# Attention scores as three products of halves, a weight conversion held behind attention's tail, and the experts' raw tiles in other places

## The chip, the core and the metric

The kernel runs on one core of a Trainium2 chip. TensorE (PE) multiplies, VectorE (DVE) and ScalarE (ACT) do the element-wise work and copy results out of PSUM, GpSimd (POOL) and SyncE (SP) mostly issue DMAs. The metric is the device time in microseconds (us): 786.6 us as the median of three runs (786.15 to 787.62).

## The reference

All inputs are float32. Three parts follow one another:

```python
scores = scale * np.matmul(q, k.transpose(0, 1, 3, 2))      # q, k, v: 2 x 12 heads x 448 x 64
scores = np.einsum('bhij,hg->bgij', scores, w_pre)          # heads are mixed before the softmax
attn = np.exp(scores - np.max(scores, axis=-1, keepdims=True))
attn = attn / (np.sum(attn, axis=-1, keepdims=True) + 1e-09)
attn = np.einsum('bhij,hg->bgij', attn, w_post)             # and after it
x = np.matmul(attn, v)                                      # as 896 tokens x 768
xn = x / np.sqrt(np.mean(x * x, axis=-1, keepdims=True) + 1e-06) * rms_g
x = (silu(xn @ w_gate) * (xn @ w_val)) @ w_out              # 768 -> 1536 -> 768
e_idx = np.argmax(x @ w_gate2, axis=1)                      # one of 8 experts for each token
out[mask] = gate_w * eom * (np.maximum(x[mask] @ w1[e], 0.0) @ w2[e])   # 768 -> 1024 -> 768
```

The weights of the feed-forward part (`w_gate`, `w_val`, `w_out`) arrive as float64 and are turned into float32 with bit operations on the chip.

## The kernel before

**Attention.** Each batch has four chunks of 120, 110, 110 and 108 query rows, eight chunks in all. A chunk's scores come from `qk` (L157): for a pair of heads, two f32 products of 64 rows each, one on each half of PE's rows, into two PSUM banks, and copies to the tile `s`. There are 48 pairs. The scores are then cut into blocks of 10 query rows x 12 heads: a DMA (`shuffle`, L166, tile `d`, 210 KB, six buffers) lays the 120 rows of a block on the partitions, on SP's queue for even blocks and on POOL's for most odd ones. There are 90 blocks. For block m, `pre` mixes the heads (L172, PE), takes the maximum (L176, DVE), `soft` exponentiates (L182, ACT), `weigh` folds the sum into the second mixing matrix `w` (L189 to L191, DVE), and `post` of block m-2 multiplies by `w` (L202, PE). Shuffles are issued five blocks ahead. The products with v (`av`, L216), the preparation of later chunks (`q_part`, `k_pair`: transposes on PE and copies) and the steps of the norm fill in the blocks. A block in the first six of a chunk also carries one pair of scores of the next chunk. The first two chunks' scores are made ahead of block 0, in `prologue`. The table `loads` says in which block each DMA of v of batch 0 (`v`, 12 heads in six parts) and of k of batch 1 is issued, on POOL's queue.

**Beside attention.** `at(m, f)` puts a step behind block m. In blocks 57 to 78 the first two columns of 128 of `w_gate` and `w_val` are loaded (L488, tile `raw`), converted by steps on DVE (L489, L490, L494) and ACT (L493), and split into a high part (fp32r, a cast on ACT, L526) and a low part (the rest, a subtraction on DVE, L527). In block 79 the third column is loaded (`load_2`), and its conversion is written behind `a.run()`; in blocks 83 to 86 the first four chunks' x are split (L475, L476). The attention itself is issued in the order written (`manual_schedule`); what stands behind it is ordered by the scheduler, which may move it ahead into attention's last blocks. `tail` is the order of what remains after the last block.

**Feed-forward part.** Every product there is made three times in fp32r, high x high, high x low, low x high (`mm3`, L502 to L504). x's two groups of 448 tokens meet 12 columns in `ffn1`; `ffn2` takes token tiles of 128 through `w_out`. `route` chooses the expert, writes the token's row to DRAM by expert, and `first_x` (L776, L784) builds the first expert's x from rows already there and from the last tile.

**Experts.** Each expert's weights are eight raw tiles of 768 KB, fetched on SP's queue (L849), cast to `wh` on ACT (L865), the rest to `wl` on DVE (L866), and used by `mm1` and `mm2` through `mm3`. `transpose_x` (L827 to L829) makes the next expert's x. The pools of raw tiles (`self.raws`) lie over memory of the feed-forward part: a tile can be fetched once its old owner is done.

## Time and profile before

| | us |
|---|---|
| median of three runs (lowest, highest) | 786.6 (786.15, 787.62) |
| the profiled execution | 786.7 |
| its span in the trace | 785.0 |
| PE busy | 730.8 (93%) |
| DVE busy | 479.8 (61%) |
| ACT busy | 387.5 (49%) |
| mean granted clock of TensorE | 0.975 |

Stage by stage: chunks 1 and 2 ahead of the blocks end at 27.7 us, attention's blocks start there, the first product of the feed-forward part is at 298.2 us, its last at 583.5, the experts follow to 785.0. The engines' shares are means over all these. A timeline row gives the start, the duration of a group of instructions, and in brackets how long the engine stood idle before them and what ended that. Rows of a matmul in f32 count two records for each instruction.

### The profile page before, as it was taken

To read this page: it belongs to the slowest core of one execution; us is meant where nothing else is said; L and a number is where in the kernel's file an instruction comes from. 1 tells how busy PE (TensorE), PEld (TensorE's weight loads), DVE (VectorE), ACT (ScalarE), POOL (GpSimd) and SP (SyncE) were. 2 spreads that over 40 slices of the span, in tenths; PEclk is the share of its full clock that TensorE was granted. 3 is DMA by queue.
4 is the path that set the end of the run, shared out by engine and by line. 5 is a ranking of instruction groups with operands and counts; after the bars stand their busy time and mean duration, and the time that the engine had idled before them with its cause. 6 is when DMAs were issued, how large, how long until landed. Compare 5 with 4: busy or idle time off the path is not lost.

```text
span 785.0 us, 11939 instructions
## 1 busy us (share of the span) xinstructions
PE 730.8 (93%) x4414; PEld 596.0 (76%) x4414; DVE 479.8 (61%) x1016; ACT 387.5 (49%) x679; POOL 78.0 (10%) x133
## 2 busy tenths in 40 slices
PE   7889999999998759999999998999988799999994
PEld 4456575665645538999999998999986688988894
DVE  3555667566775775788888823032106889778750
ACT  3455656556565453534334512232215777778661
POOL 5133100121001000000000000011000000020010
PEclk9999999999999799999999999999998899999998
DMA  8577755667566404795554000131159999999100
GB/s 136 105 157 147 121 73 82 120 121 173 86 145 113 86 5 161 205 284 195 185 176 163 1 1 0 45 138 61 41 192 387 378 380 381 380 342 355 58 25 17
DMA packets 83434, 122.02 MB, mean 155 GB/s; under 512 B 20915, under 2 KB 63559, under 8 KB 83375
## 3 DMA queue, kind: packets, MB, share of 16 engines
q1 hardware_dynamic: 75471, 98.05, 42.8%
q0 software_dynamic: 6752, 20.05, 12.3%
q10 hardware_dynamic: 1152, 3.15, 1.1%
q8 instruction: 36, 0.59, 0.3%
q14 instruction: 23, 0.19, 0.1%
HBM read 90.51 MB, written 12.21 MB: 131 GB/s over the span
## 4 chain that ended last, share of the span: by engine, by line
PE 66%; DMA 11%; DVE 9%; issue 7%; ACT 5%; POOL 0%; SPq 0%; POOLq 0%; DVEq 0%; ACTq 0%
PE ps_po L202 7%; PE ps_pm L172 6%; PE ps_pm L504 5%; PE ps_pm L502 5%; PE ps_pm L503 5%; PE ps_po L504 5%; PE ps_po L503 5%; PE ps_po L502 5%; PE ps_qk L157 4%; PE ps_av L216 4%; PE ps_qk L503 3%; PE ps_qk L504 3%; PE ps_qk L502 3%; DMA d<-s 3%; DMA xe<-ys 2%
## 5 line engine op out<-in xcount | busy, mean ns | idle before, releaser
L202 PEld LDWEIGHTS ps_po<-w,p 120*112 120x112 f32 x720 | 84.7, 180 | 68.6 <-issue 41.9
L866 DVE TENSOR_TENSOR wl<-raw,wh 128x1536 fp32r<-128x1536 f32 x64 | 110.9, 1754 | 28.2 <-ACT wh L865 28.1
L202 PE MATMUL ps_po<-w,p 120*112 120x120 f32 x720 | 94.9, 276 | 18.4 <-DVE w L191 17.1
L182 ACT ACTIVATE p<-ps_pm,mx 120x448 f32<-120x448 f32 x90 | 57.1, 634 | 102.9 <-DVE mx L176 62.0
L865 ACT CAST wh<-raw 128x1536 fp32r<-128x1536 f32 x64 | 93.0, 1481 | 7.6 <-PE ps_pm L504 4.7
L172 PE MATMUL ps_pm<-d,a_kpre 120*120 120x448 f32 x180 | 86.8, 564 | 4.9 <-DMA d<-s 4.9
L176 DVE TENSOR_REDUCE mx<-ps_pm 120x1 f32<-120x448 f32 x90 | 56.0, 622 | 49.7 <-PE ps_pm L172 49.0
L493 ACT ACTIVATE raw<-raw 128x768 f32<-128x768 f32 x36 | 33.0, 922 | 70.8 <-DVE raw L490 64.0
L204 ACT COPY at<-ps_po 112x480 f32<-112x480 f32 x90 | 50.9, 566 | 3.3 <-PE ps_po L202 1.1
L157 PE MATMUL ps_qk<-kt,qt 64*110 64x448 f32 (+2 forms) x192 | 52.1, 589 | 0.5 <-ACT qt L88 0.2
L503 PE MATMUL ps_po<-wl,hh 128*128 128x384 f32 x144 | 49.4, 343 | 0.3 <-DVE wl L866 0.2
L502 PE MATMUL ps_po<-wh,hh 128*128 128x384 f32 x144 | 49.2, 342 | 0.0
L504 PE MATMUL ps_po<-wh,hl 128*128 128x384 f32 x144 | 48.6, 340 | 0.1
L502 PE MATMUL ps_pm<-wh,xh 128*128 128x512 f32 x108 | 44.9, 416 | 3.0 <-ACT xh L828 2.2
L166 POOL DMA_DIRECT2D d<-s x42 | 24.7, 589 | 218.5 <-PE ps_pm L172 173.6
L504 PE MATMUL ps_pm<-wh,xl 128*128 128x512 f32 x108 | 44.1, 410 | 2.2 <-DVE xl L829 2.2
L216 PE MATMUL ps_av<-at,v 112*64 112x110 f32 (+2 forms) x768 | 45.0, 264 | 1.2 <-ACT at L204 0.7
L503 PE MATMUL ps_pm<-wl,xh 128*128 128x512 f32 x108 | 44.4, 411 | 1.5 <-DVE wl L866 1.5
L597 DVE TENSOR_TENSOR hl<-h,hh 128x1536 fp32r<-128x1536 f32 (+2 forms) x9 | 12.3, 1400 | 48.6 <-ACT hh L596 24.6
L216 PEld LDWEIGHTS ps_av<-at,v 112*64 112x64 f32 x768 | 37.0, 137 | 6.0 <-ACT at L204 0.9
L88 DVE COPY s<-ps_qk 110x448 f32<-110x448 f32 (+2 forms) x48 | 29.8, 622 | 14.8 <-PE ps_qk L157 13.8
L157 PEld LDWEIGHTS ps_qk<-kt,qt 64*110 64x110 f32 (+2 forms) x192 | 15.3, 174 | 30.5 <-issue 22.6
(258 smaller groups left out, 1589.1 us busy)
## 6 DMA issues: line engine op xcount, KB each, us to landing
raw<-in_moe_w_dram SPq DMA_DIRECT2D x64, 768.0 KB
d<-s SPq DMA_DIRECT2D x48, 210.0 KB
raw<-in_moe_w_gate_dram SPq DMA_DIRECT2D x12, 768.0 KB
raw<-in_moe_w_val_dram SPq DMA_DIRECT2D x12, 768.0 KB
raw<-in_moe_w_out_dram SPq DMA_DIRECT2D x12, 768.0 KB
d<-s POOLq DMA_DIRECT2D x42, 210.0 KB, 5.6
ys<-z SPq DMA_DIRECT2D x8, 385.0 KB
v<-in_v_dram POOLq DMA_DIRECT2D x12, 224.0 KB, 6.5
```

What stands on the lines that cost most here:

```text
L157: nc.tensor.matmul(pss[e][:ni], lhsT=self.qt[n][e * D:(e + 1) * D, p, :ni], rhs=self.kt[b, p][e * D:(e + 1) * D, :], start=True, stop=True,)
L172: self.marks[m, "p"] = nc.tensor.matmul(ps, lhsT=self.kpre.rearrange("p i g -> p (i g)"), rhs=self.dt.pop(m), start=True, stop=True).ins
L176: self.marks[m, "v"] = nc.vector.tensor_reduce(mx, ps, axis=AX.X, op=ALU.max, negate=True).ins
L182: self.nc.scalar.activation(p, ps, AF.Exp, bias=mx, scale=1.0, accum_out=sm)
L202: nc.tensor.matmul(ps[:, c], lhsT=p[:, c * CP:(c + 1) * CP], rhs=w, start=True, stop=True)
L204: self.marks[m + self.LP, "a"] = nc.scalar.copy(dst, ps.rearrange("p c h i -> p (c h) i")).ins
L216: nc.tensor.matmul(ps[e * D:(e + 1) * D, j, :ni], lhsT=vt[(g0 + e) // HH][:self.CP, (g0 + e) % HH, c, :], rhs=at[:, c, g0 + e, :ni], start ...
L502: nc.tensor.matmul(ps, lhsT=ah, rhs=bh, start=first, stop=False)
L503: nc.tensor.matmul(ps, lhsT=ah, rhs=bl, start=False, stop=False)
L504: self.last["t"] = nc.tensor.matmul(ps, lhsT=al, rhs=bh, start=False, stop=last).ins
L865: self.nc.scalar.copy(h, raw)
L866: self.last["v"] = self.nc.vector.tensor_sub(l, raw, h.bitcast(F32)).ins
```

## The change

It does seven things. (1) q and k are split into high and low halves when they are transposed (`k_pair`, `q_part`; the low half, a subtraction on DVE, is returned and issued a little later), and `qk` makes three fp32r products for each half of the rows. The low halves of k lie in tiles of `w0`, so the homes of the split weights swap between `nw` and `w0`. (2) v of batch 0 is loaded in blocks 6 to 16, not 0 to 10, and six parts of k of batch 1 in blocks 7 to 17 between them, the rest in 19 to 24. (3) The low halves of the first two weight columns are made one block after the high ones, as are those of x. (4) In `tail` the casts of two chunks stand ahead of their subtractions. (5) The third column's conversion waits until the last x of attention is split. (6) The first products of `first_x` are issued inside the last `route`. (7) The experts' pools are laid out anew: `hi` first, then raw tiles in pools of 1, 2, 2, 2, 4, 2, 1.

```diff
@@ -129,22 +129,29 @@
             )
-        kt = self.kp_.tile([128, self.S], F32, tag="kt", name="kt")
-        self.evict(kt, ps.rearrange("p c j -> p (c j)"))
-        self.kt[b, p] = kt
+        kt = self.kp_.tile([128, self.S], F32R, tag="kt", name="kt")
+        if p % 3 == 0:
+            self.kl = self.klo.tile([128, 1536], F32R, tag="wg" if p == 0 else "wv", name="ktl")
+        kl = self.kl[:, p % 3 * self.S:(p % 3 + 1) * self.S]
+        src = ps.rearrange("p c j -> p (c j)")
+        nc.scalar.copy(kt, src)
+        self.kt[b, p] = kt, kl
+        return lambda: nc.vector.tensor_sub(kl, src, kt.bitcast(F32))
     def q_part(self, n, j, tag="qk"):
...
         if j == 0:
-            self.qt[n] = self.qp.tile([128, self.NP, self.QB], F32, tag="qt", name="qt")
+            self.qt[n] = self.qp.tile([128, 2, self.NP, self.QB], F32R, tag="qt", name="qt", bufs=1)
         ps = self.psum(tag, [128, 3, self.QB])
...
             )
-        self.evict(self.qt[n][:, 3 * j:3 * j + 3, :ni], ps[:, :, :ni])
+        qh, ql = (self.qt[n][:, x, 3 * j:3 * j + 3, :ni] for x in range(2))
+        nc.scalar.copy(qh, ps[:, :, :ni])
+        return lambda: nc.vector.tensor_sub(ql, ps[:, :, :ni], qh.bitcast(F32))
     def qk(self, n, p):
@@ -153,11 +160,13 @@
         pss = [self.psum("qk", [self.QB, self.S]) for _ in range(2)]
-        for e in range(2):
-            nc.tensor.matmul(
-                pss[e][:ni], lhsT=self.qt[n][e * D:(e + 1) * D, p, :ni], rhs=self.kt[b, p][e * D:(e + 1) * D, :],
-                start=True, stop=True,
-            )
+        kh, kl = self.kt[b, p]
+        for x, (a, k) in enumerate(((0, kh), (0, kl), (1, kh))):
+            for e in range(2):
+                sl = slice(e * D, (e + 1) * D)
+                nc.tensor.matmul(
+                    pss[e][:ni], lhsT=self.qt[n][sl, a, p, :ni], rhs=k[sl, :], start=(x == 0), stop=(x == 2),
+                )
         return [lambda e=e: self.evict(self.st[n][:ni, 2 * p + e, :], pss[e][:ni]) for e in range(2)]
...
@@ -252,9 +261,10 @@
         self.prologue()
-        loads = {2 * j: f for j, f in enumerate(self.load_kv(0, "v"))}
-        loads.update({j + 12: f for j, f in enumerate(self.load_kv(1, "k"))})
-        avs, todo, preps = [], [], []
+        loads = {2 * j + 6: f for j, f in enumerate(self.load_kv(0, "v"))}
+        for j, f in enumerate(self.load_kv(1, "k")):
+            loads[2 * j + 7 if j < 6 else j + 13] = f
+        avs, todo, preps, lows = [], [], [], []
         for m in range(NB + LP):
@@ -264,6 +274,9 @@
                 if busy:
+                    for f in lows:
+                        f()
+                    lows = []
                     evicts = self.qk(n + 1, r)
@@ -293,10 +306,13 @@
                             avs.pop(0)()
+                    for f in lows:
+                        f()
+                    lows = []
                     if preps and m < NB and (n or r >= self.NP):
-                        preps.pop(0)()
+                        lows += filter(None, [preps.pop(0)()])
                         if len(preps) > nr - 1 - r:
-                            preps.pop(0)()
+                            lows += filter(None, [preps.pop(0)()])
                 if not avs or busy or end:
@@ -472,8 +488,14 @@
         xh, xl = (self.xs[g][:, j, :, o:o + ni] for j in range(2))
-        nc.scalar.copy(xh, x)
-        nc.vector.tensor_sub(xl, x, xh.bitcast(F32))
+
+        def high():
+            self.last["xa"] = nc.scalar.copy(xh, x).ins
+
+        def low():
+            self.last["xv"] = nc.vector.tensor_sub(xl, x, xh.bitcast(F32)).ins
+
+        return high, low
     def f64_to_f32(self, src, raw, t=None):
@@ -521,14 +543,18 @@
     def split_one(self, fc, f, nm, eng):
-        t = (self.nw if fc % 2 else self.w0).tile([128, 2, self.KD, 128], F32R, tag="w" + nm, name=nm + "hl")
+        t = (self.w0 if fc % 2 else self.nw).tile([128, 2, self.KD, 128], F32R, tag="w" + nm, name=nm + "hl")
         h, l = t[:, 0], t[:, 1]
-        self.nc.scalar.copy(h, f)
-        eng.tensor_sub(l, f, h.bitcast(F32))
-        return h, l
+        return [lambda: self.nc.scalar.copy(h, f), lambda: eng.tensor_sub(l, f, h.bitcast(F32))], (h, l)
...
...
@@ -618,7 +644,7 @@
         return ys
-    def route(self, t, y):
+    def route(self, t, y, beside=None):
         nc, E, rp = self.nc, self.E, self.rp
@@ -629,6 +655,8 @@
             nc.tensor.matmul(lg, lhsT=yT[:, k, :], rhs=self.rw[:, k, :], start=(k == 0), stop=(k == self.KD - 1))
+        if beside:
+            beside()
         v, col = nc.vector, lambda j: m[:, j:j + 1]
@@ -938,8 +966,12 @@
                 for js, some, f, nm in zip(slots, steps, fs, "gv"):
-                    some = some + [lambda f=f, nm=nm: ws[fc].append(self.split_one(fc, f, nm, nc.vector))]
-                    for m, s in zip(js, some):
+                    def split(f=f, nm=nm, m=js[6]):
+                        (high, low), hl = self.split_one(fc, f, nm, nc.vector)
+                        ws[fc].append(hl)
+                        high()
+                        at(m, low)
+                    for m, s in zip(js, some + [split]):
                         at(m, s)
@@ -959,38 +991,48 @@
                     for fc, j, tag in ((0, 0, "qk"), (0, 1, "qk"), (1, 0, "qk"), (1, 1, "pm"))]
-            late = [lambda c=c: self.split_x(c[0] * a.S + c[1], c[2]) for c in a.chunks[-4:]]
+            def late(c):
+                return self.split_x(c[0] * a.S + c[1], c[2])
             def gen():
-                n = 0
                 while todo:
                     yield todo.pop(0)
-                yield lambda: begin_x(1)
-                yield from late[:3]
+                begin_x(1)
+                cs = [late(c) for c in a.chunks[-4:]]
+                yield cs[0][0]
+                yield cs[1][0]
                 yield from avs[:3]
+                yield cs[0][1]
                 yield fill[0]
+                yield cs[1][1]
                 yield from avs[3:]
+                yield cs[2][0]
+                yield cs[2][1]
                 yield fill[1]
-                steps = [s for s in todo]
+                steps = list(todo)
                 k = [s.__name__ for s in steps].index("mean") + 1
...
                 yield from steps[k:]
-                yield late[3]
+                yield from cs[3]
             return gen()
         with ExitStack() as actx:
-            a = Attention(tc, actx, self.psum, self.ident, self.xT, self.nw, sp, self.norm, beside, tail,
+            a = Attention(tc, actx, self.psum, self.ident, self.xT, self.nw, sp, self.w0, self.norm, beside, tail,
                           self.q, self.k, self.v, self.w_pre, self.w_post)
...
             self.NCH = len(a.chunks)
-            at(57, first_weights(0, ((58, 61, 62, 63, 64, 65), (60, 63, 64, 65, 66, 67))))
-            at(68, first_weights(1, ((69, 73, 74, 74, 75, 76), (70, 75, 76, 76, 77, 78))))
+            at(57, first_weights(0, ((58, 61, 62, 63, 64, 65, 66), (60, 62, 63, 64, 65, 66, 67))))
+            at(68, first_weights(1, ((69, 73, 74, 75, 76, 77, 78), (70, 74, 75, 76, 77, 78, 79))))
             at(79, load_2)
...
             for j, c in enumerate(a.chunks[:4]):
-                at(83 + j, lambda c=c: self.split_x(c[0] * a.S + c[1], c[2]))
+                def split(c=c, j=j):
+                    high, low = self.split_x(c[0] * a.S + c[1], c[2])
+                    high()
+                    at(84 + j, low)
+                at(83 + j, split)
             with tc.manual_schedule():
@@ -1009,9 +1051,11 @@
             self.ffn1_out(fc, 0, early[fc, 0], early[fc, 1])
-        for some in raw2.pop():
-            for f in some:
-                f()
+        steps = raw2.pop()
+        with tc.issue_after(self.last["xa"]), tc.issue_after(self.last["xv"]):
+            for some in steps:
+                for f in some:
+                    f()
         self.ffn1(0, 1, ws[0])
@@ -1053,8 +1097,8 @@
         y, = self.ffn2(ts, hs)
-        part = self.first_x(xs[0])
-        self.route(self.TT - 1, y)
+        part = []
+        self.route(self.TT - 1, y, lambda: part.extend(self.first_x(xs[0])))
         self.warm(self.NW[2], self.last["t"])
@@ -1062,12 +1106,10 @@
         m2 = ExitStack()
-        self.raws = []
-        for i, n in enumerate((3, 2, 2, 6, 1)):
-            self.raws += [self.pool(m2, f"raw{i}", n)] * n
-        self.raws = self.raws[7:13] + self.raws[:7] + self.raws[13:]
+        self.hi = self.pool(m2, "hi", self.NHL)
+        self.raws = [[self.pool(m2, f"raw{i}", n)] * n for i, n in enumerate((1, 2, 2, 2, 4, 2, 1))]
+        self.raws = [p for i in (4, 0, 1, 2, 5, 3, 6) for p in self.raws[i]]
         self.nraw = 0
-        self.hi = self.pool(m2, "hi", self.NHL)
         self.xp = self.pool(m2, "xp", 2)
```

On PE, in the blocks of chunk 2 that carry scores of chunk 3 (110 rows), the products of scores stand thus before and after (`kt` and `ktl` are the high and low halves of k; the high and low halves of q are both `qt`):

```order
L157 MATMUL ps_qk<-kt,qt 110x448 x2
L202 MATMUL ps_po<-w,p 112x120 x4
L172 MATMUL ps_pm<-d,a_kpre 120x448
L157 MATMUL ps_qk<-kt,qt 110x448 x2
L202 MATMUL ps_po<-w,p 112x120 x4
```

```order
L167 MATMUL ps_qk<-kt,qt 110x448 x2
L167 MATMUL ps_qk<-ktl,qt 110x448 x2
L167 MATMUL ps_qk<-kt,qt 110x448 x2
L211 MATMUL ps_po<-w,p 112x120 x4
L181 MATMUL ps_pm<-d,a_kpre 120x448
L167 MATMUL ps_qk<-kt,qt 110x448 x2
L167 MATMUL ps_qk<-ktl,qt 110x448 x2
```

One pair of f32 products has become three pairs of fp32r products at the same place; nothing else has moved there.

On DVE, in the blocks from 79 on, the third column's conversion (`raw`) stands before:

```order
L489 TENSOR_SCALAR raw<-raw 128x768
L527 TENSOR_TENSOR vhl<-raw,vhl 128x768
L176 TENSOR_REDUCE mx<-ps_pm 120x1
L189 TENSOR_SCALAR sm<-sm 120x1
L490 SCALAR_TENSOR_TENSOR raw<-raw 128x768
L190 RECIPROCAL sm<-sm 120x1
L191 TENSOR_SCALAR w<-a_kpost,sm 120x120
L436 TENSOR_REDUCE ss<-sq 128x110
L176 TENSOR_REDUCE mx<-ps_pm 120x1
L189 TENSOR_SCALAR sm<-sm 120x1
L494 SCALAR_TENSOR_TENSOR raw<-raw 128x768
L190 RECIPROCAL sm<-sm 120x1
```

The last `w` of attention and what follows it after the change:

```order
L200 TENSOR_SCALAR w<-a_kpost,sm 120x120
L198 TENSOR_SCALAR sm<-sm 120x1
L199 RECIPROCAL sm<-sm 120x1
L200 TENSOR_SCALAR w<-a_kpost,sm 120x120
L496 TENSOR_TENSOR x_3198<-xT,x_3198 128x6x120
L496 TENSOR_TENSOR x_3198<-xT,x_3198 128x6x110
L511 TENSOR_SCALAR raw<-raw 128x768
L512 SCALAR_TENSOR_TENSOR raw<-raw 128x768
L516 SCALAR_TENSOR_TENSOR raw<-raw 128x768
L496 TENSOR_TENSOR x_3198<-xT,x_3198 128x6x110
L452 TENSOR_REDUCE ss<-sq 128x108
L460 TENSOR_SCALAR nv<-ps_av 128x108
```

No conversion step is left ahead of the last `w`; the first that now follows (`raw`, the fourth column's) stands ahead of the subtraction of a late chunk of x (`x_3198`).

On DVE, at the first two experts (`wl` of both, `hl` of the first's hidden values, `xl` of the second's x), before and then after:

```order
L866 TENSOR_TENSOR wl<-raw,wh 128x1536 x3
L896 TENSOR_TENSOR hl<-ps_qk,hh 128x512
L866 TENSOR_TENSOR wl<-raw,wh 128x1536 x2
L896 TENSOR_TENSOR hl<-ps_qk,hh 128x512
L866 TENSOR_TENSOR wl<-raw,wh 128x1536 x5
L909 TENSOR_SCALAR ids<-mt 128x1
L866 TENSOR_TENSOR wl<-raw,wh 128x1536
L829 TENSOR_TENSOR xl<-ps_qk,xh 128x512
L829 TENSOR_TENSOR xl<-ps_qk,xh 128x256
L866 TENSOR_TENSOR wl<-raw,wh 128x1536
```

```order
L894 TENSOR_TENSOR wl<-raw,wh 128x1536 x2
L924 TENSOR_TENSOR hl<-ps_qk,hh 128x512
L894 TENSOR_TENSOR wl<-raw,wh 128x1536 x2
L924 TENSOR_TENSOR hl<-ps_qk,hh 128x512
L894 TENSOR_TENSOR wl<-raw,wh 128x1536
L857 TENSOR_TENSOR xl<-ps_qk,xh 128x512
L857 TENSOR_TENSOR xl<-ps_qk,xh 128x256
L937 TENSOR_SCALAR ids<-mt 128x1
L894 TENSOR_TENSOR wl<-raw,wh 128x1536 x7
```

The second expert's `xl` has moved from behind eleven `wl` of this stretch to behind five, ahead of a run of seven.

## Rows read from the trace of the kernel before

**Rows 1.** Windows by stage: length; busy (instructions) per engine; granted clock, DMA share, GB/s.

```profile
39.20:45.80 6.60, 3.57 (x14) 2.73 (x14) 1.53 (x6) 2.05 (x6) 0.78 (x2) 0.74 0.82 180
54.00:199.50 145.50, 145.14 (x1073) 91.09 (x1072) 93.82 (x290) 85.77 (x209) 27.73 (x44) 1.00 0.69 121
249.40:298.20 48.80, 31.93 (x278) 23.47 (x274) 30.38 (x86) 25.39 (x57) 1.73 (x3) 0.90 0.28 59
298.20:583.50 285.30, 282.19 (x1539) 264.45 (x1537) 155.04 (x301) 94.25 (x151) 10.06 (x26) 0.99 0.38 122
592.00:630.00 38.00, 31.30 (x137) 26.57 (x136) 29.90 (x40) 25.43 (x25) 2.91 (x3) 0.82 1.06 381
```

**Rows 2.** Timeline of PE, early attention: start, us, engine, line, operation, count, [idle before].

```profile
42.24 1.72 PE L172 MATMUL ps_pm<-d,a_kpre 120*120 120x448 f32 x2 [3.03 <-DMA d<-s]
```

**Rows 3.** Windows by stage of the early DMA load.

```profile
22.00:34.00 12.00, 9.93 (x35) 4.05 (x35) 6.68 (x18) 5.26 (x13) 1.30 (x2) 1.00 0.56 99
34.00:44.00 10.00, 6.61 (x34) 4.29 (x33) 3.40 (x12) 3.82 (x10) 2.59 (x4) 0.92 0.85 177
```

**Rows 4.** Timeline of PE, two blocks without and with scores.

```profile
49.30 0.92 PE L172 MATMUL ps_pm<-d,a_kpre 120*120 120x448 f32 x2
50.05 1.02 PE L202 MATMUL ps_po<-w,p 120*112 120x120 f32 x8
...
54.09 0.92 PE L172 MATMUL ps_pm<-d,a_kpre 120*120 120x448 f32 x2
54.94 1.01 PE L157 MATMUL ps_qk<-kt,qt 64*110 64x448 f32 x4
55.87 1.07 PE L202 MATMUL ps_po<-w,p 120*112 120x120 f32 x8
```

**Rows 5.** Timeline of PE, first products of the feed-forward part.

```profile
298.72 0.36 PE L504 MATMUL ps_qk<-x,ghl 128*128 128x448 f32 x1
298.92 0.37 PE L502 MATMUL ps_qk<-x,ghl 128*128 128x448 f32 x1
```

**Rows 6.** Timeline of PE, scores of the second chunk ahead of the blocks.

```profile
25.15 2.62 PE L157 MATMUL ps_qk<-kt,qt 64*110 64x448 f32 x8 [0.19 <-DVE s L88]
```

**Rows 7.** Timeline of DVE, low halves of the first two weights.

```profile
212.29 0.97 DVE L527 TENSOR_TENSOR ghl<-raw,ghl 128x768 fp32r<-128x768 f32 x1 [1.53 <-ACT ghl L526]
...
219.04 0.96 DVE L527 TENSOR_TENSOR vhl<-raw,vhl 128x768 fp32r<-128x768 f32 x1 [2.70 <-ACT vhl L526]
```

**Rows 8.** Timeline of DVE, the third column's conversion in the tail.

```profile
256.32 0.56 DVE L489 TENSOR_SCALAR raw<-raw 128x768 uint32<-128x768 uint32 x1 [6.91 <-DMA raw<-in_moe_w_gate_dram]
```

**Rows 9.** Timeline of PE at the same place.

```profile
259.75 1.91 PE L202 MATMUL ps_po<-w,p 120*112 120x120 f32 x8 [7.70 <-DVE w L191]
```

**Rows 10.** Windows: the stall's stretch alone.

```profile
249.40:264.20 14.80, 7.10 (x33) 4.97 (x30) 7.30 (x17) 5.75 (x13) 0.90 (x2) 0.65 0.55 145
```

**Rows 11.** Waits of DVE in 249.4:298.2: us in total, times, longest.

```profile
DVE x L476 <- ACT x L475: 7.7, 4, 2.6
```

**Rows 12.** Timeline of DVE, start of the feed-forward part.

```profile
303.37 0.56 DVE L489 TENSOR_SCALAR raw<-raw 128x768 uint32<-128x768 uint32 x1 [4.45 <-DMA raw<-in_moe_w_gate_dram]
```

**Rows 13.** Timeline of PE, from the feed-forward part into the experts.

```profile
586.42 0.94 PE L776 MATMUL ps_pm<-ident,xe 128*128 128x128 f32 x6 [2.92 <-DMA xe<-ys]
...
596.35 0.50 PE L502 MATMUL ps_pm<-wh,xh 128*128 128x512 f32 x1 [0.78 <-ACT wh L865]
...
620.52 0.50 PE L502 MATMUL ps_pm<-wh,xh 128*128 128x512 f32 x1 [2.22 <-ACT xh L828]
...
623.89 0.79 PE L504 MATMUL ps_pm<-wh,xl 128*128 128x512 f32 x1 [2.18 <-DVE xl L829]
```

**Rows 14.** The page's costliest groups: busy, mean ns, idle before.

```profile
L866 DVE TENSOR_TENSOR wl<-raw,wh 128x1536 fp32r<-128x1536 f32 x64 | 110.9, 1754 | 28.2 <-ACT wh L865 28.1
```

**Rows 15.** Timeline of DVE, low half of the second expert's rows.

```profile
623.15 1.01 DVE L829 TENSOR_TENSOR xl<-ps_qk,xh 128x512 fp32r<-128x512 f32 x2
```

**Rows 16.** The chain that ended last: start, us, what.

```profile
611.52 9.87 DMA raw<-in_moe_w_dram
```

More of the change, by code (lines that the diff above doesn't have):

```diff
@@ L28, with __init__ @@
     SH, LP = 5, 2
-    def __init__(self, tc, ctx, ps, ident, xT, nat, sp, on_chunk, beside, tail, q, k, v, w_pre, w_post):
+    def __init__(self, tc, ctx, ps, ident, xT, nat, sp, klo, on_chunk, beside, tail, q, k, v, w_pre, w_post):
         self.tc, self.nc, self.ident, self.xT = tc, tc.nc, ident, xT
@@ L243, in prologue @@
             self.shuffle(m)
-        self.q_part(1, 0, "av")
-        self.q_part(1, 1, "qk")
+        self.q_part(1, 0, "av")()
+        self.q_part(1, 1, "qk")()
         for p in range(self.NP):
@@ L577, in split_wo @@
         homes = [(p, "raw" + g) for p in (self.nw, self.w2p, self.w0) for g in "gv"]
-        homes += [(p, "w" + g) for p in (self.w0, self.nw) for g in "gv"]
+        homes += [(p, "w" + g) for p in (self.nw, self.w0) for g in "gv"]
         if k < len(homes):
```

18 lines of the change are left out of this document (12 added, 6 removed).

## The prediction

> **What bounds the kernel now.** The profiled execution took 786.7 us (span 785.0); the three timed runs have a median of 786.6, so sums made against the trace need no correction. I read the windows by stage first. From 54 to 199.5 us PE is busy 145.14 of 145.5 us, and in the feed-forward part (298.2 to 583.5) 282.19 of 285.3 [rows 1]: there only less PE work can help. PE idles in three places: the early blocks (3.57 us busy of 6.6), attention's tail (31.93 of 48.8) and the first experts (31.30 of 38.0), and in each the granted clock is lower too, 0.74, 0.90 and 0.82 [rows 1]. Those are the places to look at; then the timelines there, for what ends each wait.
>
> **Early loads.** Before block 6 PE waits 3.03 us for a shuffled tile (`d<-s`), and the block's first product then takes 1.72 us for two records [rows 2], against 0.92 in a later block [rows 4]: the lower of the two clock levels, 1.2 GHz. A clock of 0.74 over 6.6 us makes about 6.6 x 0.26 x 2 = 3.4 us at that level, of which half, 1.7 us, is lost. The shuffles share the DMA engines there with v of batch 0: from 22 to 34 us 99 GB/s move, from 34 to 44 us 177 [rows 3], so the shuffles were slowed by load, not by their count. The change sends v 6 blocks later. Gain: 2.9 (the 3.03, less a rest) + 1.7 = 4.6 at most. Against it: k of batch 1 now lies between v's parts, and in blocks 6 to 11 about 175 KB/us would be asked for, as much as both queues moved together [rows 3]; a v that lands late would stall the weighted sums, or a shuffle again. I take 4 us, bounds -2 to 4.6; -2 is most of a wait like the present one, come again later at full clock.
>
> The Trainium skill, "DMA: Bandwidth & Descriptors", section "Rules for kernel authors", says that spreading transfers over issuing engines gives no bandwidth, since they interleave on the same 16 DMA engines. By it, what leaves blocks 0 to 5 comes back in 6 to 17; the row is against the strict form, since 177 GB/s with both queues is well over 99 with one, so the rule has its chance only as a rival below.
>
> **Scores.** 48 pairs of f32 products become 48 x 3 pairs of fp32r products on the row halves. An f32 product of 448 columns takes 0.75 us (49.30 to 50.05), and the four records of one pair of halves 0.93 to the next line (54.94 to 55.87) [rows 4]. Two products in 0.93 can only be if the halves run side by side: a slot of 0.75 and some 0.18 for the change of shape. An fp32r product of 448 columns starts 0.20 after the one before it [rows 5], so three slots are 0.61 and the pair saves 0.14. 36 of the pairs lie in blocks where PE has no idle time [rows 1]: 36 x 0.14 = 5 us. The other 12 I count at nothing: the second chunk's last two pairs ahead of the blocks take 2.62 us, 1.3 each, well over a slot, and follow a wait for DVE's copy [rows 6]. With all 48 the gain would be 6.8. No row shows an fp32r product of 64 rows. If its halves do not run side by side, six slots make 1.21 against 0.75: 36 x -0.47 = -17. I take +5, as the f32 rows of the same shape do run side by side. The extra work, a cast on ACT and a subtraction on DVE for each of 12 k tiles and 16 q parts, is hidden: in 54 to 199.5 DVE is busy 93.8 and ACT 85.8 of 145.5 us [rows 1]; without that cover it is about 0.5 us a part.
>
> The Trainium skill, "TensorEngine Tiling (Array Packing)", section "PSUM Bottleneck", says that tiling speeds up the products but not the copies out of PSUM, which may then set the pace. The chunk ahead of the blocks agrees [rows 6]; in the blocks the copies' engines have a third of their time left, so I hold it for a rival.
>
> **First two weight columns (blocks 57 to 79).** Each half's DVE step waits 1.53 and 2.70 us for ACT's cast of the same tile [rows 7], with the softmax queued behind it on DVE. The change puts the low half one block later. 4.2 us are there at most; PE has other products beside part of it, so 2, bounds 0 to 4.2.
>
> **Attention's tail.** The scheduler had put the third column's conversion ahead of the softmax: DVE waits 6.91 us for its DMA [rows 8], with `w` of a block behind it, and PE waits 7.70 us for that `w` [rows 9]. In 14.8 us the clock is 0.65 [rows 10], that is 14.8 x 0.35 x 2 = 10.4 us at 1.2 GHz, up to 264.2; from 259.75 on PE works in it, 4.45 us of which 2.2 are lost. After, no conversion step is in DVE's row before the last `w`; the wait goes. What is late next is DVE on ACT's cast in the splitting of x, 7.7 us in four waits [rows 11], of which the deferred low halves should give PE something. Lower bound 7.5: the stall alone, nearly all of it. Upper 13.3: 7.7 + 2.2 + 3.4, somewhat under half of those 7.7. I take 7.7 + 2.2 + 1.1 = 11. The conversion's steps (0.56 and some 0.95 us each) now stand at the start of the feed-forward part. DVE waited 4.45 us there for the fourth column's raw tile [rows 12]; in the new order that column's steps stand ahead of a late low half of x. PE has early products to run beside it; I take -0.8, bounds -2.5 to 0 (about half of that wait).
>
> **Into the experts.** Five raw tiles, not two, can now be fetched during the feed-forward part, because their homes lie over tensors that come free early; and x of the second expert is transposed in the middle of the first's second product, not behind it. Before, PE waits 2.22 and 2.18 us for that x (620.52, 623.89) [rows 13], and a raw tile that lands at 611.52 + 9.87 = 621.4 is on the chain [rows 16]. From 623.89 to the window's end at 630 the clock is low: a product takes 0.79 us, not 0.50 [rows 13], so 2.3 to 3.0 of 6.1 us are lost (by the durations, or by half), say 2.7. Four products were done by 623.89, about 0.9 us of work, so the second expert's stream stands as if it had begun at 623.9 + 2.7 - 0.9 = 625.7 and never stopped. After, DVE sets the pace: from about 595 (the first product is at 596.35 [rows 13]) nine low halves at 1.754 [rows 14] make 15.8, and the low halves of x (1.01 for each of two [rows 15]) and of h (by their columns two thirds of that, twice) 3.4: 614.2, with 0.8 for ACT's casts 615. Gain 10.7, taken as 11. Upper bound: two of the nine are done before 595, since their tiles are there by then, 14.2. Lower: the tiles land as late as before and of the two waits 3 us go. The wait of 2.92 us for the gathered rows [rows 13] stays. The five early tiles cost nothing beside a feed-forward part in which the DMA engines are 0.38 busy [rows 1].
>
> **Sum.** 4 + 5 + 2 + 11 - 0.8 + 11 = 32.2; 786.7 - 32.2 = 754.5 us.
>
> **Rivals.**
> - Experts start no earlier: DMA is at 381 GB/s from 592 to 630 [rows 1], so the order of tiles may only shift which is late. For it: the landing on the chain [rows 16]. Against: the low halves of DVE wait 28.1 us for ACT, not for DMA [rows 14]. Term 3 for 11: 762.5.
> - The scores gain nothing since copies or the change of shape set their pace: 754.5 + 5 = 759.5. For: rows 6; against: rows 1.
> - The moved loads take back what they give, term 0: 758.5.
> - Another wait replaces the tail's: DVE and ACT alternate on softmax and x [rows 11], so only 3 of 11 come: 762.5.
> - The fp32r halves run one after the other: 754.5 + 22 = 776.5; with the other terms at their low ends as well, no change.
> - Slower: an fp32r product on a row half takes a whole f32 slot and is not paired. Six records of 0.376 are 2.26 against 0.75, 48 x 1.51 = 72 us in all 48 pairs: 786.7 - 27.2 + 72 = 831.5. It decides from 1.32 us a pair (27.2 / 48 = 0.57 over 0.75). For it: no row shows the shape. Against: fp32r at 0.20 on whole rows [rows 5] and the f32 halves in pairs [rows 4].
>
> **How the numbers follow.** Forecast 0.63; experts 0.12; scores nothing 0.06; loads 0.06; tail 0.05; halves in turn 0.04; slower 0.04. About 0.2% is what a measurement of this kernel tells from no change. Only the last case is slower; of the halves-in-turn case a quarter, 0.01, ends within 0.2%. Faster is the rest, 0.95. The likeliest case's own range is 746 (early terms, tail and experts near their upper bounds) to 763; with the rivals of 758.5 to 762.5 and two of them together it is 746 to 768, which leaves the last two cases and mixtures outside.
>
> **What would show it.** Right: block 6 starts near 39 us with no clock dip at 42; a block's scores hold PE 0.79 us, not 0.93; DVE has no wait of 7 us for a weight's DMA in the tail and the clock stays up there; the feed-forward part starts near 276 us (298.2 - 22); the second expert's first products have no 2 us waits and start some 19 us after the first's, not 24. Wrong: a pair of scores of 1.2 us or more; a new wait of PE for v, or for `d<-s`, between blocks 6 and 17; DVE waiting for the fourth column's raw tile with x's low half behind it for more than 2.5 us; the raw tile of the second expert still landing after 620 on the old scale.

## The result and the profile after

The changed kernel takes 753.82 us (median of four runs, 753.48 to 755.22), against 787.01 (786.15 to 787.62) for the kernel before: a ratio of 0.9582, 95% interval 0.9566 to 0.9599. The prediction said 754.5. The profiled execution took 753.48 us, its span is 751.7, and the mean granted clock is 0.986.

The gain is read most plainly by laying the starts of the same instruction in the two traces side by side (the gain is the difference):

| start of | before, us | after, us | gained so far |
|---|---|---|---|
| block 0 | 27.70 | 27.66 | 0.04 |
| block 12 | 54.09 | 50.43 | 3.66 |
| block 57 | 183.09 | 177.31 | 5.78 |
| block 80 | 251.13 | 241.07 | 10.06 |
| first product of the feed-forward part | 298.21 | 276.68 | 21.53 |
| end of the feed-forward part | 583.50 | 562.18 | 21.32 |
| first expert's first product | 596.35 | 570.67 | 25.68 |
| second expert's first product | 620.52 | 592.80 | 27.72 |
| third expert's first product | 643.91 | 611.20 | 32.71 |
| end of the span | 784.98 | 751.75 | 33.23 |

This is one pair of executions. In a second trace of the changed kernel (e12) block 12 starts at 52.80 us, 2.37 later than here, the first product of the feed-forward part at 277.00, only 0.32 later, and the span is 751.7 again. So the total repeats better than the stages it is made of.

The windows by stage, set to the stages of the new trace (columns as in [rows 1]):

```profile
39.20:45.80 6.60, 5.54 (x37) 4.39 (x38) 3.69 (x13) 4.04 (x12) 3.35 (x5) 1.00 0.84 168
239.40:276.70 37.30, 31.24 (x277) 23.30 (x275) 26.27 (x79) 22.40 (x52) 1.73 (x3) 0.95 0.33 78
276.70:562.20 285.50, 282.57 (x1541) 264.97 (x1540) 159.04 (x307) 97.06 (x154) 10.44 (x26) 0.99 0.40 129
570.70:608.00 37.30, 35.61 (x180) 31.12 (x179) 35.44 (x38) 33.10 (x34) 8.43 (x1) 0.95 1.06 381
```

In the early window PE is busy 5.54 of 6.6 us where it was 3.57, at full clock (in e12 4.84 us, at 0.74 of it). The tail is 37.30 us long where it was 48.80, with nearly the same work (31.24 against 31.93 us busy; 0.95 of the clock against 0.90: from 269.9 to 273.3 us the granted clock is at its lower level). The feed-forward part is as long as it was. In the experts' first 37 us PE is busy 35.61 us.

The timeline of PE at blocks 5 and 6, in place of [rows 2]:

```profile
37.24 0.98 PE L181 MATMUL ps_pm<-d,a_kpre 120*120 120x448 f32 x2 [1.13 <-ACT at L213]
40.26 0.98 PE L181 MATMUL ps_pm<-d,a_kpre 120*120 120x448 f32 x2 [1.22 <-ACT at L213]
```

In this execution there is no wait for the shuffle `d` at these two blocks. PE still waits 1.13 and 1.22 us, now for ACT's copy `at` of an earlier block; the first product takes 0.98 us, so the clock is up. The wait is not gone for good: e1 below has the other executions.

The timeline of PE in a block with scores, in place of the second half of [rows 4]:

```profile
50.43 0.92 PE L181 MATMUL ps_pm<-d,a_kpre 120*120 120x448 f32 x2
51.28 0.46 PE L167 MATMUL ps_qk<-kt,qt 64*110 64x448 f32 x2
51.58 0.38 PE L167 MATMUL ps_qk<-ktl,qt 64*110 64x448 f32 x2
51.78 0.37 PE L167 MATMUL ps_qk<-kt,qt 64*110 64x448 f32 x2
52.09 1.07 PE L211 MATMUL ps_po<-w,p 120*112 120x120 f32 x8
```

Three rows of two products each, 0.30, 0.20 and 0.31 us from one to the next, where one row of four records took 0.93. From 51.28 to 52.09 it is 0.81 us, and every such block is 0.14 shorter. But behind the sixth pair of a chunk some of that is given back. In block 40 PE waits for ACT's copy of the last scores (`s`), 0.46 us after the change (first row) where it was 0.17 (second row, the kernel before):

```profile
130.82 1.04 PE L211 MATMUL ps_po<-w,p 120*112 120x120 f32 x8 [0.46 <-ACT s L88]
136.04 1.04 PE L202 MATMUL ps_po<-w,p 120*112 120x120 f32 x8 [0.17 <-ACT s L88]
```

Blocks 51, 63 and 74 have the same wait, each 0.29 or 0.30 us longer than before, and e12 repeats all four. At the first such place, ahead of block 18, this trace has a wait of 0.31 us for DVE's `w`; e12 has none there.

The low halves of the first column on DVE, in place of [rows 7], follow their neighbours with no idle time:

```profile
205.70 0.96 DVE L548 TENSOR_TENSOR ghl<-raw,ghl 128x768 fp32r<-128x768 f32 x1
...
208.43 0.95 DVE L548 TENSOR_TENSOR vhl<-raw,vhl 128x768 fp32r<-128x768 f32 x1
```

In the tail (239.4 to 276.7 us) the waits of PE for `w`, and of DVE for ACT's cast of x, in place of [rows 9, 11]; no row of DVE waits for a weight's DMA there:

```profile
PE ps_po L211 <- DVE w L200: 4.5, 5, 1.5
```

```profile
DVE x L496 <- ACT x L493: 4.0, 1, 4.0
```

The start of the feed-forward part on DVE, in place of [rows 12]: the fourth column's raw tile is waited for about as long as before, 4.65 us, and the low half of x behind it (second row) comes 3.5 us later:

```profile
281.29 0.56 DVE L511 TENSOR_SCALAR raw<-raw 128x768 uint32<-128x768 uint32 x1 [4.65 <-DMA raw<-in_moe_w_gate_dram]
...
284.76 0.85 DVE L496 TENSOR_TENSOR x<-xT,x 128x660 fp32r<-128x660 f32 x1
```

The way into the experts on PE, in place of [rows 13]:

```profile
562.34 0.39 PE L804 MATMUL ps_pm<-ident,xe 128*128 128x128 f32 x2
...
570.67 0.47 PE L524 MATMUL ps_pm<-wh,xh 128*128 128x512 f32 x1
572.83 0.50 PE L525 MATMUL ps_pm<-wl,xh 128*128 128x512 f32 x1 [1.69 <-DVE wl L894]
...
592.80 0.39 PE L524 MATMUL ps_pm<-wh,xh 128*128 128x512 f32 x1
```

There is no wait for the gathered rows `xe` at 562.34, one of 1.69 us for the first `wl`, and none at the second expert's products (592.80).

### The profile page after: what moved, and what is told of

Its sections match the earlier page's. It is cut to its first block, busy times and chain, and to the rows that moved or that the text cites. A ratio compares the mean times of both kernels' runs of the same rounds, so it can differ in the third digit from the quotient of the medians.

```text
span 751.7 us, 12181 instructions
## 1 busy us (share of the span) xinstructions
PE 717.7 (95%) x4510; PEld 601.7 (80%) x4510; DVE 484.6 (64%) x1030; ACT 393.7 (52%) x693; POOL 84.3 (11%) x133
## 4 chain that ended last, share of the span: by engine, by line
PE 79%; DVE 7%; issue 6%; DMA 3%; ACT 2%; SPq 1%; POOL 0%; POOLq 0%; DVEq 0%; ACTq 0%
PE ps_po L211 8%; PE ps_pm L181 7%; PE ps_pm L526 7%; PE ps_pm L525 7%; PE ps_pm L524 7%; PE ps_po L526 6%; PE ps_po L524 6%; PE ps_po L525 6%; PE ps_av L225 5%; PE ps_qk L167 4%; PE ps_qk L526 3%; PE ps_qk L525 3%; PE ps_qk L524 3%; DVE mx L185 1%; PE ps_av L657 1%
## 5 line engine op out<-in xcount | busy, mean ns | idle before, releaser
L181 PE MATMUL ps_pm<-d,a_kpre 120*120 120x448 f32 x180 | 85.2, 556 | 3.9 <-ACT at L213 2.3
L167 PE MATMUL ps_qk<-kt,qt 64*110 64x448 f32 (+2 forms) x192 | 41.8, 418 | 2.5 <-ACT s L88 2.3
L167 PEld LDWEIGHTS ps_qk<-kt,qt 64*110 64x110 f32 (+2 forms) x192 | 18.3, 175 | 31.8 <-issue 20.1
L938 POOL DMA_INDIRECT out_dram<-o,ids x9 | 19.7, 2190 | 149.1 <-ACT o L935 132.9
```

Source lines behind the costliest of these rows:

```text
L167: nc.tensor.matmul(pss[e][:ni], lhsT=self.qt[n][sl, a, p, :ni], rhs=k[sl, :], start=(x == 0), stop=(x == 2),)
L181: self.marks[m, "p"] = nc.tensor.matmul(ps, lhsT=self.kpre.rearrange("p i g -> p (i g)"), rhs=self.dt.pop(m), start=True, stop=True).ins
```

## The experiments

Times differed more between the executions here than between those that gave the result (the kernel before, timed again beside the experiments, had medians of 787.15, 785.82 and 786.89 us, and single runs from 782 to 791). What a run tells is therefore read mostly from its trace, from the starts of the same instructions stage by stage. Where two traces have the same code, the difference that the early blocks gave them stays the same from block 19 to block 89, within 0.15 us. Behind block 89 it does not, because the granted clock falls there in some executions and not in others. From block 89 to the first product of the feed-forward part, e1, e6, e8, e9 and e12, which have the changed kernel's code there, take 9.60 or 9.61 us at full clock. The changed kernel's profiled run takes 11.03, of which 3.4 us are at the lower level, and e7 12.44, with 6.8.

### e1: the old loads

```diff
-        loads = {2 * j + 6: f for j, f in enumerate(self.load_kv(0, "v"))}
-        for j, f in enumerate(self.load_kv(1, "k")):
-            loads[2 * j + 7 if j < 6 else j + 13] = f
+        loads = {2 * j: f for j, f in enumerate(self.load_kv(0, "v"))}
+        loads.update({j + 12: f for j, f in enumerate(self.load_kv(1, "k"))})
```

Expected: 

> The changed kernel with v of batch 0 and k of batch 1 loaded in their old blocks. Theory (the loads' move buys the early stage alone): block 12 starts 3.6 us later, PE waits about 3 us for a shuffled tile before block 6 and the clock falls there again; 757.4 us. Rival (the wait moves to a later block and the loads take back what they give): less than 1 us slower, 754 to 754.8.

756.68 us, ratio 0.962 (0.9592 to 0.9648). The wait before block 5 is back, and the half clock behind it (PE's timeline; 1.82 us for two records):

```profile
39.43 0.98 PE L181 MATMUL ps_pm<-d,a_kpre 120*120 120x448 f32 x2 [3.05 <-DMA d<-s]
...
42.55 1.82 PE L181 MATMUL ps_pm<-d,a_kpre 120*120 120x448 f32 x2 [0.94 <-DMA d<-s]
```

From block 0 to block 12 it takes 27.4 us, in the profiled run of the changed kernel 22.8. But that run was the shortest of its kind. In ten traces with the loads moved this stretch took 22.8, 23.2, 23.4, 23.9, 24.0, 24.2, 24.3, 24.6, 24.6 and 25.6 us, mean 24.1; in four with the old loads (this one, the kernel before, e10 and e11) 27.4, 26.4, 26.5 and 24.4, mean 26.1. So the size is about 2 us in the mean, with executions that overlap, not the 3.66 of the one pair of traces.

The mechanism is the expected one only in part. With the loads moved, nine of the ten traces still have a wait for `d` before block 6, of 1.3 to 2.8 us; it is missing in the changed kernel's first trace alone. All waits for `d` between block 0 and block 12 together are 0.5 to 4.6 us, against 4.1 to 4.9 with the old loads. What differs more clearly is the clock: with the old loads it is at its lower level for 3.4 or 6.8 us of this stretch in each of the four traces, with the loads moved in two of ten (e6 and e12). In e12, the changed kernel itself, the wait and the slow product behind it are both there:

```profile
40.96 1.75 PE L181 MATMUL ps_pm<-d,a_kpre 120*120 120x448 f32 x2 [2.48 <-DMA d<-s]
```

### e2: the scores in f32; e8: the halves one behind the other

```diff
-        kh, kl = self.kt[b, p]
-        for x, (a, k) in enumerate(((0, kh), (0, kl), (1, kh))):
-            for e in range(2):
...
+        for e in range(2):
+            nc.tensor.matmul(
+                pss[e][:ni], lhsT=self.qt[n][e * D:(e + 1) * D, p, :ni], rhs=self.kt[b, p][e * D:(e + 1) * D, :],
+                start=True, stop=True,
+            )
```

with `k_pair` and `q_part` as before. Expected: 

> The changed kernel with q, k and the scores in f32 as before. Theory (36 pairs in full blocks save 0.143 us each, 5.1, of which some 1.7 are given back in the blocks behind each chunk's sixth pair, where PE meets the copies): 757.2 us, and the blocks behind the sixth pair no longer lose 0.3. Rival 1 (the loss behind the sixth pair has nothing to do with the scores): 758.9. Rival 2 (the extra halves cost as much as the products save): 753.8.

757.07 us, ratio 0.9627 (0.9598 to 0.9656). The pair takes 0.93 us again (PE's timeline):

```profile
53.31 1.01 PE L159 MATMUL ps_qk<-kt,qt 64*110 64x448 f32 x4
54.24 1.07 PE L204 MATMUL ps_po<-w,p 120*112 120x120 f32 x8
```

Between block 12 and block 80 this kernel loses 3.50 us on the changed one, as expected: 36 x 0.143 = 5.1 less what the blocks behind the sixth pair give back. Those blocks no longer lose (0.30 us back at block 64 alone). The pair of traces before and after gives 3.3 over the same blocks (10.06 - 3.66, less the 3.1 that e11 shows for the weights). So the scores are worth 3.3 to 3.5 us.

```diff
-        for x, (a, k) in enumerate(((0, kh), (0, kl), (1, kh))):
-            for e in range(2):
+        for e in range(2):
+            for x, (a, k) in enumerate(((0, kh), (0, kl), (1, kh))):
```

Expected: 

> The changed kernel with the three products of one row half behind those of the other, not in turn. Theory (only neighbours on different halves run side by side): six slots of 0.20 in place of three, 36 x 0.61 = 22 us slower, 775.8. Rival (PE runs the halves side by side whatever the order): 753.8.

755.47 us, ratio 0.9609 (0.9559 to 0.966), and a span of 751.7, the changed kernel's own. PE's timeline in block 12:

```profile
52.55 0.46 PE L167 MATMUL ps_qk<-kt,qt 64*110 64x448 f32 x2
52.84 0.37 PE L167 MATMUL ps_qk<-ktl,qt 64*110 64x448 f32 x2
53.05 0.37 PE L167 MATMUL ps_qk<-kt,qt 64*110 64x448 f32 x2
53.35 1.07 PE L211 MATMUL ps_po<-w,p 120*112 120x120 f32 x8
```

The records start as they did with the halves in turn, pair beside pair, though the program names the second half's products behind all of the first's. The theory is wrong and the rival right: products on the two row halves ran side by side here without being neighbours in the program.

### e3, e10, e11: what took the tail's stall away

```diff
-        with tc.issue_after(self.last["xa"]), tc.issue_after(self.last["xv"]):
-            for some in steps:
-                for f in some:
-                    f()
+        for some in steps:
+            for f in some:
+                f()
```

Expected: 

> The changed kernel without the hold on the third column's conversion, so that the scheduler puts it back among attention's last blocks. Theory (the stall was the wait for its DMA on DVE, with the softmax behind): PE waits 6 to 8 us in block 80, the clock falls, 7.7 + 2.2 less the 0.8 at the feed-forward's start: 762.9 us. Rival (with x's halves apart, DVE has room for the steps and the DMA is there in time): 754 to 756.

758.0 us, ratio 0.9655 (0.9596 to 0.9713). The conversion is back among the last blocks, but DVE waits only 2.0 and 0.8 us for its DMAs:

```profile
DVE raw L511 <- DMA raw<-in_moe_w_gate_dram: 2.0, 1, 2.0
DVE raw L511 <- DMA raw<-in_moe_w_val_dram: 0.8, 1, 0.8
```

Between blocks 82 and 84 the kernel loses 2.2 us, and little more up to its end: a quarter of what was expected, so the theory fell. In this program's order DVE takes the first conversion step behind block 81's maximum, not ahead of block 80's as in the kernel before, and the DMA has more time to land. Two runs on the kernel before take the two suspects one at a time. e10 adds only the hold:

```diff
...
+        steps = raw2.pop()
+        with tc.issue_after(self.last["xa"]), tc.issue_after(self.last["xv"]):
+            for some in steps:
...
```

Expected: 

> The kernel before with only the hold on the third column's conversion. Theory (the stall is DVE's wait for that DMA, and the hold alone takes it away): block 81 starts 8 us sooner, about 9 us faster in all, 777.5 us. Rival (without the later low halves another wait takes its place in blocks 79 to 82): less than 3 us, 784 to 787.

780.36 us, ratio 0.9914 (0.9888 to 0.9941). Block 81 starts 5.9 us sooner (its gain on the kernel before goes from -1.10 at block 80 to 4.79), and that stays to the end. PE's waits for `w` in 235 to 292 us:

```profile
PE ps_po L202 <- DVE w L191: 10.5, 8, 2.2
```

e11 makes only the low halves of the first two columns one block later (some steps ahead of them move by a block too):

```diff
-                    some = some + [lambda f=f, nm=nm: ws[fc].append(self.split_one(fc, f, nm, nc.vector))]
...
+                        nc.scalar.copy(h, f)
+                        at(m, lambda: nc.vector.tensor_sub(l, f, h.bitcast(F32)))
...
-            at(57, first_weights(0, ((58, 61, 62, 63, 64, 65), (60, 63, 64, 65, 66, 67))))
+            at(57, first_weights(0, ((58, 61, 62, 63, 64, 65, 66), (60, 62, 63, 64, 65, 66, 67))))
```

Expected: 

> The kernel before with only the low halves of the first two weight columns made one block later. The scheduler then puts the third column's conversion two blocks later by itself. Theory (this move alone takes most of the stall, as where the hold was undone): DVE's wait for the DMA falls from 6.9 to about 2 us, with the 3 us of the blocks up to 79 some 9 us faster, 778 us. Rival (the stall needs the hold): only the 3 us up to block 79, 784 us.

780.09 us, ratio 0.9918 (0.9883 to 0.9952). It gains 3.1 us from block 57 to 80, then 8.5 at block 81, and loses 3.9 of them by block 84, where DVE now waits:

```profile
DVE raw L489 <- DMA raw<-in_moe_w_gate_dram: 2.1, 1, 2.1
```

So each edit alone takes over half of the 8.6 us that blocks 80 to 84 gained: the hold 5.7, the later low halves 4.7 (by moving the conversion in the scheduler's order), the whole change 8.6. Neither theory nor rival of e10 had that right in size. Of e11 the theory holds for the wait (2.1 us) and nearly for the gain (8.1 us by the traces, 6.8 by the medians, 9 expected).

### e4 and e5: the low halves at once

```diff
                         high()
-                        at(m, low)
+                        low()
```

for the weights, with the old slots. Expected: 

> The changed kernel with the low halves of the first two weight columns made at once and the old slots. Theory (DVE waits for ACT's cast with the softmax behind it): blocks 67 to 79 lose 3.1 us together and 756.9 us. Rival (that wait lies beside PE's other products and the gain there came from the slots of the steps, or from nothing that lasts): less than 1 us, 753.8 to 754.8.

760.36 us, ratio 0.967 (0.9636 to 0.9703): a larger loss than expected. From block 57 to 79 the trace loses 2.3 us, near the expected 3.1. Another 1.5 go by block 82, where the last low half, now in block 78, has the softmax behind it (first row, PE's timeline), and 2.3 more between block 89 and the first product of the feed-forward part, at the lower clock level (the last two):

```profile
249.21 1.04 PE L211 MATMUL ps_po<-w,p 120*112 120x120 f32 x8 [2.20 <-DVE w L200]
...
276.77 3.51 PE L211 MATMUL ps_po<-w,p 120*112 120x120 f32 x16 [1.52 <-DVE w L200]
280.99 4.59 PE L225 MATMUL ps_av<-at,v 112*64 112x108 f32 x48 [0.71 <-ACT at L213]
```

The same two groups in the changed kernel, 3.35 and 2.44 us:

```profile
270.24 3.35 PE L211 MATMUL ps_po<-w,p 120*112 120x120 f32 x16 [1.53 <-DVE w L200]
274.31 2.44 PE L225 MATMUL ps_av<-at,v 112*64 112x108 f32 x48 [0.71 <-ACT at L213]
```

In both the clock falls while PE stands idle in the tail; here it stays low for 10.2 us, there for 3.4. In the changed kernel's second trace (e12) PE stands idle just as long, 1.52 us, and the clock does not fall:

```profile
271.98 1.93 PE L211 MATMUL ps_po<-w,p 120*112 120x120 f32 x16 [1.52 <-DVE w L200]
```

So these last 2.3 us can't be put down to the edit; the 3.8 us up to block 82 can. Why the clock stayed low longer here is not settled.

```diff
                     high()
-                    at(84 + j, low)
+                    low()
```

and the same in `tail`. Expected: 

> The changed kernel with the low halves of x made at once, in the blocks and in the tail. Theory (the tail's gain is the conversion's stall, and the halves add the small rest): 1 to 2 us slower, 755.3. Rival 1 (PE gets back all of what the four waits of DVE for ACT showed at most, 3.4): 757.2. Rival 2 (nothing): 753.8.

758.65 us, ratio 0.9642 (0.9617 to 0.9667). DVE's four waits for ACT's cast are back as in [rows 11], and PE's for `w` are 8.7 us, not 4.5:

```profile
DVE x L496 <- ACT x L493: 7.8, 4, 2.6
```

```profile
PE ps_po L211 <- DVE w L200: 8.7, 7, 2.0
```

From block 84 to the first product of the feed-forward part this trace takes 24.27 us, as the kernel before does (24.25) and e10 (24.24). The changed kernel takes 21.42 in its profiled run, with 3.4 us at the lower clock, and 19.99 in e12, where the clock is at its full level throughout, as it is in e5. Compared at full clock the deferred halves are worth 4.3 us, which is also what PE's waits for `w` differ by (4.2). That is more than the theory (1 to 2) and than rival 1 (3.4): PE gets over half of DVE's 7.8 us back.

### e6, e7, e9: the way into the experts

```diff
-        self.hi = self.pool(m2, "hi", self.NHL)
-        self.raws = [[self.pool(m2, f"raw{i}", n)] * n for i, n in enumerate((1, 2, 2, 2, 4, 2, 1))]
-        self.raws = [p for i in (4, 0, 1, 2, 5, 3, 6) for p in self.raws[i]]
+        self.raws = []
+        for i, n in enumerate((3, 2, 2, 6, 1)):
+            self.raws += [self.pool(m2, f"raw{i}", n)] * n
+        self.raws = self.raws[7:13] + self.raws[:7] + self.raws[13:]
```

Expected: 

> The changed kernel with the experts' pools of raw tiles as before. Theory (two tiles instead of five ahead of the experts make the first two experts late by the 7.5 us that lie between the first expert's first product and the third expert's): 761.3 us. Rival (the gain came from the first rows' products inside the last routing and from the earlier transposes, which stay): 754 to 756.

760.21 us, ratio 0.9651 (0.9598 to 0.9704). From the end of the feed-forward part to the end of the span the trace is 6.0 us longer (7.5 expected). The waits of PE from there to the second expert:

```profile
PE ps_pm L524 <- ACT xh L856: 2.2, 1, 2.2
PE ps_pm L526 <- DVE xl L857: 2.0, 1, 2.0
PE ps_pm L804 <- DMA xe<-ys: 1.7, 1, 1.7
```

Both waits of [rows 13] for the second expert's x are back, and one for `xe`, which the prediction had let stand whatever was done. In e6 the DMA of `xe` is issued at 559.15 us, 0.84 behind the first raw tile (558.31); in the changed kernel at 557.39, 0.12 ahead of it (557.51). Two other traces with the new pools lie between: issued 0.15 us behind that tile (e4), the rows keep PE waiting 0.6 us; issued 0.05 behind (e5), they show no wait.

```diff
-        part = []
-        self.route(self.TT - 1, y, lambda: part.extend(self.first_x(xs[0])))
+        part = self.first_x(xs[0])
+        self.route(self.TT - 1, y)
```

Expected: 

> The changed kernel with the first rows' products ahead of the last routing again. Theory (PE, at the head of its queue, waits for the gathered rows, and the routing behind it is late by the same): 756.7 us, the 2.9 us wait back. Rival (the rows land in time by themselves, since the raw tiles no longer go ahead of them): 754.5, only the order of some 1.5 us of products.

757.08 us, ratio 0.9619 (0.9565 to 0.9674). The trace loses nothing from the end of the feed-forward part on (its lag on the changed kernel goes from 4.72 us to 4.23 at the last expert), and PE waits for `xe` only this long:

```profile
PE ps_pm L804 <- DMA xe<-ys: 0.3, 1, 0.3
```

The rival is right in that the rows land in time with the pools laid anew. That the place of their products buys nothing is not shown: up to the first expert the clock stays up in e7, where both traces of the changed kernel have 3.4 us at the lower level. In e2, which has the changed kernel's code there and a clock that stays up too, the first expert begins 7.50 us behind the end of the feed-forward part, in e7 8.69. With the old pools (e6) it is 8.74, and in the kernel before 12.85, with 3.4 us at the lower level: as in the tail, either edit alone takes most of it.

The changed kernel still shows a row of waits there, ACT's casts of the first expert's `wh` for their raw tiles:

```profile
568.74 1.47 ACT L893 CAST wh<-raw 128x1536 fp32r<-128x1536 f32 x1 [1.30 <-DMA raw<-in_moe_w_dram]
...
576.99 1.48 ACT L893 CAST wh<-raw 128x1536 fp32r<-128x1536 f32 x1 [1.47 <-DMA raw<-in_moe_w_dram]
```

Idle time of 1.30 us ahead of the first, 0.70 and 0.55 ahead of the next two, and 1.47 ahead of the fourth (second row): the homes that come free early go to the first expert's second matrix. e9 turns that round.

```diff
-        self.raws = [p for i in (4, 0, 1, 2, 5, 3, 6) for p in self.raws[i]]
+        self.raws = [p for i in (0, 1, 2, 4, 5, 3, 6) for p in self.raws[i]]
```

Expected: 

> The changed kernel with the raw tiles' pools taken in another order, 0, 1, 2, 4, 5, 3, 6 and not 4, 0, 1, 2, 5, 3, 6, so that the first expert's first matrix lies in the homes that come free early and is fetched first. Theory (ACT's casts of that matrix wait some 4 us for its DMAs, and DVE and PE behind them): the casts are done during the last routing, the first expert's products run without gaps, the second expert starts 3 to 4 us sooner; 751 us. Rival 1 (DVE's row of low halves sets the pace anyway): 753.8. Rival 2 (the second matrix now comes late): 755.

and the changed kernel beside it, expected: 

> The changed kernel once more, beside the one with the other order of raw tiles. Both theories: 753.8 us; its early blocks show how far the start differs between executions: block 12 between 22.5 and 25.6 us behind block 0.

e9: 751.62 us, ratio 0.9559 (0.9515 to 0.9603). The changed kernel again: 754.61, ratio 0.9602 (0.9557 to 0.9648). ACT casts two tiles of `wh` before the feed-forward part has ended:

```profile
558.74 2.86 ACT L893 CAST wh<-raw 128x1536 fp32r<-128x1536 f32 x2 [1.24 <-PE ps_po L526]
```

and of PE's waits behind it only the one of the last routing (1.0 us) and this one are left:

```profile
PE ps_po L525 <- DVE wl L894: 0.2, 1, 0.2
```

Between the end of the feed-forward part and the second expert's first product this kernel gains 4.0 us on the changed one in the trace, and keeps 3.5 to the end. The theory holds. The two intervals overlap, so by timing alone the 3 us between the medians are not settled; by the trace they are there.

## Why the prediction was right

The total (754.5 against 753.82) rests on terms of which most were near, with errors of both signs inside them. That they cancel to 0.7 us is in part luck.

- **Early loads, 4.** The pair of traces gives 3.66, the mean over all traces about 2 (e1). The step that the wait of 3.03 us goes, but for a rest, did not hold: nine of ten traces keep 1.3 to 2.8 us of it. The lower clock behind it is what mostly went. The size was taken from one execution of a stretch that varies by some 3 us.
- **Scores, 5.** The saving of a block was right to 0.01 us (0.143 against 0.14), and so was the choice that the halves run side by side. What was missing is what the blocks behind each sixth pair give back: 3.3 to 3.5 us remain. That the copies' engines have a third of their time left was true over the whole stretch, and yet it is a copy, ACT's of the last scores, that PE waits for there, some 0.3 us longer than before. The rival drawn from the Trainium skill's "TensorEngine Tiling (Array Packing)", section "PSUM Bottleneck", was a third right.
- **First two weight columns, 2.** 3.1 from block 57 to block 80 when made alone (e11), within 0 to 4.2; undone, the blocks up to 79 lose 2.3 (e4).
- **Tail, 11.** 11.5 from block 80 to the first feed-forward product, made up otherwise than forecast. The stall and its clock gave 8.6 (blocks 80 to 84), not 9.9, and the hold was not their one cause: e3, e10 and e11 show two edits, either of which takes over half of it. The deferred halves of x gave 4.3 at full clock (e5), not 1.1, more than even the upper bound allowed them (3.4). And the sign that the clock stays up failed in the profiled execution: its fall took 1.4 us back, which e12 does not lose.
- **Start of the feed-forward part, -0.8.** -0.2: the low half of x did come behind the fourth column's tile, and the part became no more than 0.2 us longer.
- **Experts, 11.** 11.9, again with steps that made up for each other. The second expert's first product was put at 615 on the old scale, 593.7 on the new one (less 21.3), and starts at 592.80 without a wait. But the first expert, which the forecast left where it was, starts 4.4 us sooner. One reason is that the sentence on the 2.92 us wait for the gathered rows, that it stays, was wrong: their DMA is no longer issued behind a raw tile (e6, e7). And the second starts 22.1 us behind the first, not "some 19". "After, DVE sets the pace" is not what the trace shows at that point: DVE is done with the second expert's x 3 us before PE begins on it (the row below), and PE is held by its own products, 3.4 us of which run at the lower clock.

```profile
588.76 1.02 DVE L857 TENSOR_TENSOR xl<-ps_qk,xh 128x512 fp32r<-128x512 f32 x2
```

Of the rivals, none decides. The slower one needed 1.32 us a pair of scores; it is 0.81. Nor do the moved loads cost anything later: from block 12 to block 40 PE shows no wait for v or `d`, in either trace of the changed kernel.

## What to carry to other kernels

Read the gain of each edit from its own stage, and lay the starts of the same instruction in two traces side by side to check it. Do so with more than one trace of each kernel: two traces of the changed kernel agree in the total and differ by 2.4 us in the early blocks and by 1.4 in the tail. When a stall goes, undo each edit from the new kernel and also make it alone on the old one: here two edits each removed over half of one stall, and making only one of them alone would have credited it with what the other takes as well. A buffer that comes free early should hold the data that is needed first (e9).

## What the runs showed of the hardware

- Products on the two halves of PE's rows ran side by side in fp32r as in f32, also when all three of one half stood ahead of all three of the other: 0.30, 0.20 and 0.30 us from pair to pair either way (e8, beside the changed kernel).
- Around the change from the whole array to row halves and back PE took a little longer: three slots of 0.20 us took 0.81 us, and the step from the mixing product to the scores 0.85 us where it is 0.76 to the next product of whole rows. That the change of shape is the reason is a reading; no run makes it alone.
- The same early blocks took 22.8 to 25.6 us in ten executions with the same order of loads, with waits for shuffles of 0.5 to 4.6 us. Such a stretch can't be sized from one trace.
- With the same code and the same idle time of PE (1.52 or 1.53 us), the granted clock fell to its lower level at the end of attention's tail in some executions and not in others: not at all in e12 (9.61 us from block 89), for 3.4 us in the changed kernel's first trace (11.03), for 6.8 in e7 (12.44).
- A gather of rows issued on ACT's queue kept PE waiting longer the further it came behind a raw tile of 768 KB on SP's: 1.7 us at 0.84 us behind (e6), 0.6 at 0.15 (e4), none at 0.12 ahead (the changed kernel).
